# Making the first tail slot's first layer in the last steps of an attention loop

## The chip, the cores and the metric

The kernel runs on one core of one Trainium2 chip. The metric is the device time of one execution in microseconds (us); the time given for a kernel is the median of its runs. Engines are called as in the profile: PE (TensorE matmul), PEld (its weight loads), DVE (VectorE), ACT (ScalarE), POOL (GpSimd), SP (SyncE, here only a DMA queue).

## The reference, cut to what matters

Attention over 8 batches of 8 heads, 576 tokens and 64 columns a head, in which each row keeps its 32 largest scores; then a mixture of 8 experts over the 4608 tokens of 512 columns, one expert for each token.

```python
scores = scale * np.matmul(q, k.transpose(0, 1, 3, 2))
kth = np.partition(scores, -top_k, axis=-1)[..., -top_k:-top_k + 1]
scores = np.where(scores >= kth, scores, -1e9)
attn = softmax(scores) ; x = np.matmul(attn, v) as [4608, 512]
logits = x @ w_gate + modality_bias[modality_id]
e_idx = np.argmax(logits, axis=1)
for e in range(E):                       # E = 8, w1[e] is 512 x 1024, w2[e] 1024 x 512
    h = np.maximum(x[mask] @ w1[e], 0.0)
    out[mask] = gate_w[mask, None] * (h @ w2[e])
```

## The kernel before, in words

**One software pipeline over 288 score tiles.** A step `i` of the loop at L1123 works on nine stages of different tiles of 128 x 576 scores: the scores of tile i+2 (`qk`, L437), the search for the 32nd largest value (L452 to L498), the exponential (`expo`, L503), `keep` (L509, on DVE, tile i-7), the transposes `trans` (L524) and their copy `evac` (L532, tile i-9) and, three times in nine steps, the product with v (`av`, L552, copied at L556). NT is 288, QL is 2, TL is 9; the loop has 310 steps. The last scores are issued in step 285, the last `trans` in step 296, the last `av` in step 297. Steps 299 to 309 hold only what makes the last batch's routing.

**Routing of the last batch**, by steps: gate logits on PE in step 299 (`logits`, L606), their copy on ACT at the head of step 300 (L607), transposes in step 300 (`logit_rows`, L615), DVE reductions in step 301 (L618 to L626), then the list of `route` (L629) with up to four small operations a step from step 302 (L666 to L685; `ranks`, L642, has PE, ACT, POOL and DVE work), `xrow` (L588, copied by ACT at L596, multiplied on POOL at L592) in steps 302 to 306. From step 309 the rows are sent to their experts' lists in DRAM by five indirect DMAs on POOL (`send`, L659, tensor `xs`).

**Experts come in slots of 256 rows.** Slots 0 to 11 are worked in the loop by a list of PE items with costs (`expert`, L814; `moe` holds them): first layer `hid` (L859), second layer `outp` (L871, 16 items of 0.88). A budget `spare_pe` gains 3.25 in each step (`STEP`, L31), less the step's own cost, and items are issued while it is above zero (L1221 to L1241). The gain falls to 1.0 from step NT+TL+END[0] on (L66, L1221). Between slots, `turns` (L798, PE at L807) may transpose the next slot's rows early.

**Seven tail slots (12 to 18) follow the loop.** They multiply in three rounded terms: weights and rows are split into a high and a low part by `parts` (L1013: ACT copy at L1015, DVE subtraction at L1016). `first` (L1121) holds the five pieces that slot 12 needs ahead: four `split_w1` and one `turn_rows` (L1026, PE at L1031); before, they go out in steps 299 to 303, after `open_tail` (L994, step 298) has closed the pools of the attention and opened the pool of the tail. `slot(n)` (L1060) works slot n-1: eight pieces of the first layer (twelve matmuls each at L1069, then ACT L1071 and DVE L1072, and at every second piece `split_w2`), the loads of slot n's weights and rows (`load_w1` L790, `fetch` L1049, whose DMA is L771), the second layer's first half (L1087), then `turn_rows(n)`, `choose(n + 1)`, and the second layer's second half. The rows that `fetch` reads for slot 13 are in `xs`, so they need the sends of the last batch, and slot 13's expert is chosen (`choose`, L1043) after the routing.

**Order.** The program is scheduled by hand: each engine's queue has its instructions in the order in which the Python text issues them. SP has all weight and row loads in one queue. PSUM tiles named X rotate through three buffers, E has one.

Of the kernel before, what the change touches and what calls it, by code (L numbers as in the profile page):

```python
# [9 lines left out]
FT = mybir.dt.float32  # L10
FR = mybir.dt.float32r
BF = mybir.dt.bfloat16
I32 = mybir.dt.int32
AF = mybir.ActivationFunctionType
# [8 lines left out]
ME = 11  # L23
# [39 lines left out]
RXM = (5, 6, 7, 8, 9)  # L63
EZP = 1
RKP = 0
END = (-3, 1.0)  # L66
BIG = float(2.0 ** 100)
EPS = 1e-9
KTH_MIN, KTH_MAX = 1e-18, float(2.0 ** 26)
# [5 lines left out]
def kernel(  # L75
# [33 lines left out]
    att = ExitStack()  # L109
    ld = att.enter_context(tc.tile_pool(name="ld", bufs=2))  # L110
    wk = att.enter_context(tc.tile_pool(name="wk", bufs=3))

    ZROW = E * LCAP
    xs = dr.tile([ZROW + SLOT, XW], FT, name="xs")
# [14 lines left out]
    def load(p, what, b=None, queues=(SP, SP, SP), bufs=None):  # L129

        o = LD.setdefault(p, {})
        h0 = 2 * (p % HP)
        for nm in what:
            src = {"k": k, "q": q, "v": v}[nm]
            g = src[p // HP] if b is None else src[ds(b, 1)].rearrange("o h s d -> (o h) s d")
            if nm == "k":
                o["kq"] = bufs["kq"] if bufs else ld.tile([128, 2, D], FT, name="kqt", bufs=1)
            t = vtb[p % 2] if nm == "v" else o["kq"][:64] if nm == "k" else o["kq"][64:]
            m = bufs[nm] if bufs else ld.tile([128, 2, 4, D] if nm == "v" else [128, 4, 2, D], FT, name=nm + "m", bufs=2 if nm == "v" else 1)
            if nm == "v":  # L140
                SP.dma_start(m.rearrange("p h c d -> p h (c d)"),
                             g[h0:h0 + 2, 0:512, :].rearrange("h (p c) d -> p h (c d)", c=4))
            else:
                for h in range(2):
                    queues[h].dma_start(m[:, :, h, :], g[h0 + h, 0:512, :].rearrange("(p c) d -> p c d", c=4))
            if nm == "v":
                tail = g[h0:h0 + 2, 512:, :].rearrange("h p d -> p h d")
                SP.dma_start(t[:64, 0:3:2, :], tail)
                SP.dma_start(t[64:, 1, :], g[h0 + 1, 512:, :])
            else:  # L150
                queues[2].dma_start(t, g[h0:h0 + 2, 512:, :].rearrange("h p d -> p h d"))
            o[nm] = (m, t)
# [136 lines left out]
    def new_st():  # L289

        if not stt:
            stt.append(wk.tile([128, 2, 2, S], FR, name="st", bufs=1))
        return stt[0]

    def keep_st(f, w, c):
# [43 lines left out]
    def stacks(p, part, late):  # L339

        d = PR[p]
        if part == "k":
            d["ks"] = wk.tile([128, 2, 2, S], FR, name="ks", bufs=2)
        else:
            d["qs"] = wk.tile([128, 2, S], FR, name="qs", bufs=2)
        for h in range(2):
            late.append(lambda h=h: stack(p, part, h))

# [22 lines left out]
    def first_pair():  # L371

        d = PR.setdefault(0, {})
        st = d["st"] = new_st()
        (km, kt), (qm, qt) = LD[0]["k"], LD[0]["q"]
        pk, pa, pq = (psX.tile([128, 512], FT, name="X") for _ in range(3))

        def turn(ps, a, m, first=False, rows=slice(0, 128)):
            PE.matmul(ps[:, a:a + rows.stop - rows.start], m, idf[rows, rows], start=first, stop=False,
                      is_transpose=True, skip_group_check=True)  # L380

        def cut(which, a, b, ps):
            hi, lo = (st[:, x, which, a:b] for x in range(2))
            A.activation(hi, ps, AF.Copy)
            V.tensor_tensor(lo, ps, hi.bitcast(FT), op=OP.subtract)

        for c in range(4):
            turn(pk, c * 128, km[:, c], c == 0)
        idle_work(4)
        turn(pa, 0, qm[:, 0], True)  # L390
        turn(pa, 128, kt, rows=slice(0, 64))
        cut(0, 0, 512, pk)
        cut(1, 0, 128, pa[:, :128])
        cut(0, 512, S, pa[:, 128:192])
        for c in range(1, 4):
            turn(pq, c * 128 - 128, qm[:, c], c == 1)
        turn(pq, 384, qt, rows=slice(64, 128))
        d["ks"] = wk.tile([128, 2, 2, S], FR, name="ks", bufs=2)
        d["qs"] = wk.tile([128, 2, S], FR, name="qs", bufs=2)
        return lambda: cut(1, 128, S, pq[:, :S - 128])  # L400

    def first_stacks():
# [591 lines left out]
    def open_tail():  # L994

        nonlocal att, wk, gt, tk
        att.close()
        att = ExitStack()
        wk = att.enter_context(tc.tile_pool(name="tl", bufs=1))
        for t, nm, shape in ((w1s, "w1", [128, KC, F]), (w2s, "w2", [128, FC, Dm]), (xgs, "xg", [128, KC, SLOT]),  # L1000
                             (hs, "h", [128, FC, SLOT])):
            t.extend(wk.tile(shape, FR, name=nm + x) for x in "hl")
        gt = wk.tile([128, 2], FT, name="gt")
        tk = const.tile([128, 2], I32, name="tk")

    TERMS = ((0, 0), (0, 1), (1, 0))
    turn = [0]
# [47 lines left out]
    def put(t, ot):  # L1055
        apart(G.indirect_dma_start(  # L1056
            out=out[:, :], out_offset=bass.IndirectOffsetOnAxis(ap=tk[:, t:t + 1], axis=0),
            in_=ot, in_offset=None, bounds_check=N - 1, oob_is_err=False), outs)

    def slot(n, between=None, early=None):  # L1060

        if last:
            last.pop()()
        of_rows(n - 1)
        for f in range(FC):
            ps = acc([128, SLOT])
            for c in range(KC):
                for x, (a, b) in enumerate(TERMS):
                    PE.matmul(ps, w1s[a][:, c, f * 128:(f + 1) * 128], xgs[b][:, c, :],  # L1069
                              start=(c == 0 and x == 0), stop=(c == KC - 1 and x == 2))  # L1070
            A.activation(hs[0][:, f, :], ps, AF.Relu)  # L1071
            V.scalar_tensor_tensor(hs[1][:, f, :], ps, 0.0, hs[0][:, f, :].bitcast(FT), op0=OP.max, op1=OP.subtract)  # L1072
            if f % 2 == 0:
                split_w2(f // 2)
            if f == 0:
                for g in range(4):
                    load_w1(n, g)
                fetch(n)
            if f % 2 == 0:
                load_w2(n, f // 2)  # L1080
        if early:
            early()
        for t in range(2):
            py = acc([128, Dm])
            for f in range(FC):
                for x, (a, b) in enumerate(TERMS):
                    PE.matmul(py, hs[a][:, f, t * 128:(t + 1) * 128], w2s[b][:, f, :],  # L1087
                              start=(f == 0 and x == 0), stop=(f == FC - 1 and x == 2))
                if t == 0 and f % 2 == 1:
                    split_w1(f // 2)  # L1090
            ot = ol if t else const.tile([128, Dm], FT, name="ot", bufs=2)
            A.activation(ot, py, AF.Copy, scale=gt[:, t:t + 1])
            if t == 1:
                last.append(lambda: put(1, ot))
            else:
                put(0, ot)
                if between:
                    between()
                turn_rows(n)
                choose(n + 1)  # L1100
# [19 lines left out]
    rows_of = {}  # L1120
    first = deque([lambda g=g: split_w1(g) for g in range(4)] + [lambda: turn_rows(nslot[0])])  # L1121
    weaving[0] = True
    for i in range(LAST):  # L1123
        if 12 <= i < 12 + 2 * E and i % 2 == 0:
            pad_rows((i - 12) // 2)
# [94 lines left out]
            keep_warm(NW)  # L1220
        spare_pe = min(spare_pe + (STEP if i < NT + TL + END[0] else END[1]) - cost, CAP)  # L1221
        while seen[0] and spare_pe > 0:
            if i < NT + ME:
                more_moe()
            o = SL.get(nslot[0])
            if i < NT + ME and plan["ready"] == nslot[0] and plan["go"] and 0 < len(moe) <= TA and "rowed" in o and "px" not in o:
                o["px"] = None
                turnq.extend(turns(nslot[0]))
            if turnq and (not turnq[0][2] or taken[0] <= 2 - ranking[0]):
                c, f, new = turnq.popleft()  # L1230
                f()
                spare_pe -= c
                continue
            if not moe:
                break
            c, f, new = moe[0]
            if taken[0] > 2 - ranking[0] if new == 2 else new and after:
                break
            moe.popleft()
            f()  # L1240
            spare_pe -= c  # L1241
# [68 lines left out]
            x[0] -= 1  # L1310
        while puts and puts[0][0] <= 0:
            puts.popleft()[1]()
        if i == NT + OPEN:
            open_tail()
        if i > NT + OPEN and first and plan["ready"] == nslot[0] and len(moe) < (16 if len(first) > 1 else 6):
            first.popleft()()
    weaving[0] = False
    chores()
    while rush:
# [59 lines left out]
    with ExitStack() as nest:  # L1379
        for x in range(MAXSLOT):  # L1380
            nest.enter_context(tc.If(nrem > x))
            slot(S0 + 3 + x)
    att.close()


    att = ctx.enter_context(ExitStack())
# [3 lines left out]
    def slow_tile(j, dn):  # L1390
# [12 lines left out]
        A.activation(ex, t["S"], AF.Exp, bias=nm_)  # L1403
        probs(j)
        V.scalar_tensor_tensor(t["P"], t["S"], m[:, 31:32], ex, op0=OP.is_ge, op1=OP.mult, accum_out=dn)

    def slow():
        Pb[:] = [wk.tile([128, 2 * S], FT, name=f"P{i}", bufs=1) for i in range(2)]
# [77 lines left out]
```

## Time and profile before

| what | value |
|---|---|
| median of 3 runs | 1245.73 us (1243.84 to 1247.1) |
| profiled execution, its own time | 1242.61 us |
| span of the profiled execution | 1240.7 us |
| mean granted TensorE clock | 0.986 |
| PE busy, PEld busy | 1176.3 us (95%), 927.6 us (75%) |
| DVE busy | 1148.1 us (93%) |
| ACT busy | 1015.7 us (82%) |
| POOL busy | 614.5 us (50%) |

The span is what lies between the first and the last instruction; the execution's time has 1.9 us around it. Shares are means over the whole span, which has an attention part (to about 1047 us), the routing of the last batch and the tail slots (1060 to 1226 us). A row of a timeline gives start, length, engine, line, operation, the tiles written and read, and in brackets the idle time before it with what ended it. Matmul records overlap, since their ends are modelled: the time that a run of matmuls takes is read from start to start.

### The profile page before, as it was taken

Reading aid. Unit: us, or ns where it says so; the run is one execution under the profiler, and the core shown is the slowest. Engines: PE = TensorE matmul, PEld = TensorE weight load, DVE = VectorE, ACT = ScalarE, POOL = GpSimd, SP = SyncE. Lnnn points to the kernel's source line nnn. Section 1 sums busy time; section 2 is a strip of 40 time slices with the busy share of each in tenths; the row PEclk is TensorE's granted clock in tenths of the full one; section 3 lists DMA queues with packets and bytes.
Section 4 is the critical chain, followed back from the end, with each engine's and each line's share of the span. In section 5 each row is a group of like instructions: output and inputs, shape, how many; then the busy total and the mean of one; then the engine's idle time right before and its main releaser. Section 6 shows DMA issues by size and latency. Waiting matters only on the chain. (4 is left out here: it accounts for less than half of the span.)

```text
span 1240.7 us, 29108 instructions
## 1 busy us (share of the span) xinstructions
PE 1176.3 (95%) x8149; PEld 927.6 (75%) x8149; DVE 1148.1 (93%) x5829; ACT 1015.7 (82%) x2044; POOL 614.5 (50%) x1054
## 2 busy tenths in 40 slices
PE   7789988899999999999999999999999999899995
PEld 6677766777767687877868687777868785799894
DVE  6999999999999999999999999999999995867763
ACT  4899988888889998899988998899889986456453
POOL 3444447445664566456754585556555662511111
PEclk8999989999999999999999999999999999999998
DMA  6687644645466456666476466756675434667563
GB/s 145 175 237 191 152 105 125 212 134 164 95 204 188 123 160 201 179 159 168 106 223 187 108 188 185 199 146 180 174 201 156 116 117 146 207 243 259 182 234 112
DMA packets 214421, 210.52 MB, mean 170 GB/s; under 512 B 108605, under 2 KB 157757, under 8 KB 214240
## 3 DMA queue, kind: packets, MB, share of 16 engines
q1 hardware_dynamic: 206672, 188.33, 54.3%
q0 software_dynamic: 6208, 19.54, 4.3%
q8 instruction: 70, 1.15, 0.4%
q14 instruction: 111, 0.91, 0.2%
q10 hardware_dynamic: 1360, 0.59, 0.2%
HBM read 130.43 MB, written 28.95 MB: 128 GB/s over the span
## 5 line engine op out<-in xcount | busy, mean ns | idle before, releaser
L452 DVE MAX8 cand<-Ssb 128x8 f32<-128x82 f32 (+1 forms) x2016 | 429.2, 230 | 7.6 <-ACT Ssb L445 7.6
L485 POOL TENSOR_TENSOR y<-Ssb,K 128x576 f32<-128x576 f32 x288 | 367.1, 1275 | 9.5 <-ACT K L479 9.0
L437 PE MATMUL S<-ks,qs 128*128 128x288 f32 x1016 | 232.3, 351 | 31.1 <-ACT Ssb L445 22.0
L445 ACT ACTIVATE Ssb<-S 128x576 f32<-128x576 f32 (+1 forms) x289 | 190.0, 658 | 71.8 <-PE S L437 56.4
L479 ACT ACTIVATE K<-Ssb,mg 128x576 bf16<-128x576 f32 x288 | 228.5, 793 | 6.0 <-POOL y L485 5.6
L503 ACT ACTIVATE ex<-Ssb,mg 128x576 f32<-128x576 f32 x288 | 227.1, 789 | 0.3 <-POOL mg L470 0.3
L437 PEld LDWEIGHTS S<-ks,qs 128*128 128x128 f32 x1016 | 157.5, 191 | 89.3 <-issue 37.1
L513 POOL TENSOR_SCALAR spare<-P 1x1 f32<-1x1 f32 x256 | 47.1, 184 | 342.6 <-DVE mg L463 326.8
L489 DVE MAX8 mg<-y 128x8 f32<-128x576 f32 x288 | 214.4, 745 | 0.9 <-POOL y L485 0.9
L509 DVE SCALAR_TENSOR_TENSOR P<-Ssb,kth,ex 128x576 f32<-128x576 f32 x256 | 211.4, 826 | 2.2 <-ACT ex L503 1.9
L532 ACT ACTIVATE PT<-T 128x640 f32<-128x640 f32 (+1 forms) x288 | 192.2, 667 | 8.6 <-PE T L524 8.6
L859 PE MATMUL E<-xgT,w1b 128*128 128x256 f32 x768 | 187.8, 385 | 3.0 <-ACT hT L863 1.3
L871 PE MATMUL E<-w2b,hT 128*128 128x512 f32 x384 | 184.8, 602 | 1.0 <-ACT ot L881 0.5
L524 PE MATMUL T<-idf,P 128*128 128x128 f32 x1152 | 169.4, 274 | 0.0
L859 PEld LDWEIGHTS E<-xgT,w1b 128*128 128x128 f32 x768 | 137.8, 190 | 28.3 <-ACT hT L863 3.0
L552 PE MATMUL X<-PT,vm 128*64 128x256 f32 (+1 forms) x1536 | 148.3, 336 | 4.2 <-issue 2.7
L524 PEld LDWEIGHTS T<-idf,P 128*128 128x128 f32 x1152 | 135.8, 140 | 4.2 <-issue 1.7
L552 PEld LDWEIGHTS X<-PT,vm 128*64 128x64 f32 x1536 | 86.3, 138 | 51.1 <-issue 19.1
L871 PEld LDWEIGHTS E<-w2b,hT 128*128 128x128 f32 x384 | 65.5, 190 | 52.9 <-issue 47.5
L592 POOL TENSOR_TENSOR x<-x,rd 128x256 f32<-128x256 f32 (+1 forms) x80 | 52.2, 659 | 30.1 <-ACT x L596 27.4
L479 ACT ACTIVATION_READ_ACCUMULATOR K<-Ssb,mg 128x1 f32 x288 | 62.3, 216 | 0.0
L463 DVE MAX8 mg<-cand 128x8 f32<-128x56 f32 x288 | 61.2, 213 | 0.2
(213 smaller groups left out, 2184.9 us busy)
## 6 DMA issues: line engine op xcount, KB each, us to landing
w1b<-in_moe_w_dram SPq DMA_DIRECT2D x80, 512.0 KB, 5.5
w2b<-in_moe_w_dram SPq DMA_DIRECT2D x80, 512.0 KB, 4.7
ks<-st SPq DMA_DIRECT2D x56, 288.0 KB, 3.6
qs<-st SPq DMA_DIRECT2D x110, 144.0 KB, 2.7
ks<-st SPq DMA_DIRECT2D x54, 256.0 KB, 4.8
xg<-xs SPq DMA_DIRECT2D x20, 516.0 KB, 5.4
vm<-in_v_dram SPq DMA_DIRECT2D x32, 256.0 KB, 4.5
km<-in_k_dram SPq DMA_DIRECT2D x55, 128.0 KB, 4.1
```

Of the source, the lines that this page charges most:

```text
L437: PE.matmul(ps[:, hf, u - a:v - a], l, d["ks"][:, x, h, u + o:v + o], start=(n == 0), stop=(n == len(terms) - 1), skip_group_check=(j == 8))
L452: return [lambda s=s: V.max(c[:, s * 8:s * 8 + 8], T[i]["S"][:, bnd[s]:bnd[s + 1]]) for s in range(NSUB)]
L479: A.activation(t["K"], t["S"], AF.Sign, scale=-1.0 - 2.0 ** -23, bias=t["mg"][:, x, 23:24], accum_out=t["n"][:, x:x + 1])
L485: G.tensor_tensor(t["y"], t["S"], t["K"], op=OP.mult)
L489: V.max(t["mg"][:, i % 3, 24:32], t["y"])
L503: A.activation(t["ex"], t["S"], AF.Exp, bias=t["mg"][:, i % 3, 0:1])
L509: V.scalar_tensor_tensor(t["P"], t["S"], kth[:, i:i + 1], t["ex"], op0=OP.is_ge, op1=OP.mult, accum_out=dn)
L524: PE.transpose(T[i]["pt"][:, x, :], (Pm if c == 4 else Pb[c % 2])[:, h * 512 + x * 128:h * 512 + x * 128 + 128], idf)
L532: A.activation(o, T[i]["pt"][:, :n], AF.Copy)
L552: PE.matmul(o.rearrange("p (a b) -> p a b", a=2) if j < 8 else o, l, r, start=(c == 0), stop=(c == 4), skip_group_check=True)
L859: PE.matmul(ps[:, f % 2], w1b[:, c, f * 128:(f + 1) * 128], xgT[:, c, :], start=(c == 0), stop=(c == KC - 1))
L871: PE.matmul(o["py"], hT[:, f, t * 128:(t + 1) * 128], w2b[:, f, :], start=(f == 0), stop=(f == FC - 1))
```

## The change

Tiles from which q and k are made (`kqt`, `km`, `qm`, `st`, `ks`, `qs`) move into a pool `pp` of their own at the right end of memory. After step NT-QL (286) `open_right` closes it and opens `tr` there, with the rounded w1 and rows of the tail slots. The five pieces of `first` may go out from step 287 on, one a step, once slot 12 is planned, fewer than 16 items of `moe` are left and no load is queued. When `first` and `moe` are empty, one piece of slot 12's first layer, `hidden(f)`, is issued at the end of each step after step 298; `slot` then skips those that were made. The gain of 3.25 lasts through step 298 (`END`). The early `turns` of a slot are tried only before step 286, and no new slot is planned once `first` has begun.

```diff
-END = (-3, 1.0)
+END = (2, 1.0)
...
+    make = ExitStack()
+    pp = make.enter_context(tc.tile_pool(name="pp", bufs=1, side="right"))
...
-            stt.append(wk.tile([128, 2, 2, S], FR, name="st", bufs=1))
+            stt.append(pp.tile([128, 2, 2, S], FR, name="st", bufs=1))
...
-        wk = att.enter_context(tc.tile_pool(name="tl", bufs=1))
-        for t, nm, shape in ((w1s, "w1", [128, KC, F]), (w2s, "w2", [128, FC, Dm]), (xgs, "xg", [128, KC, SLOT]),
-                             (hs, "h", [128, FC, SLOT])):
+        wk = att.enter_context(tc.tile_pool(name="tl", bufs=1, reuse_waits="tile"))
+        for t, nm, shape in ((w2s, "w2", [128, FC, Dm]), (hs, "h", [128, FC, SLOT])):
...
+    def open_right():
+
+        make.close()
+        tr = make.enter_context(tc.tile_pool(name="tr", bufs=1, side="right", reuse_waits="tile"))
+        for t, nm, shape in ((w1s, "w1", [128, KC, F]), (xgs, "xg", [128, KC, SLOT])):
+            t.extend(tr.tile(shape, FR, name=nm + x) for x in "hl")
...
+    def hidden(f):
+        ps = acc([128, SLOT])
+        for c in range(KC):
+            for x, (a, b) in enumerate(TERMS):
+                PE.matmul(ps, w1s[a][:, c, f * 128:(f + 1) * 128], xgs[b][:, c, :],
+                          start=(c == 0 and x == 0), stop=(c == KC - 1 and x == 2))
+        A.activation(hs[0][:, f, :], ps, AF.Relu)
+        V.scalar_tensor_tensor(hs[1][:, f, :], ps, 0.0, hs[0][:, f, :].bitcast(FT), op0=OP.max, op1=OP.subtract)
+        if f % 2 == 0:
+            split_w2(f // 2)
...
-            if i < NT + ME:
+            if not first_begun[0]:
                 more_moe()
...
-            if i < NT + ME and plan["ready"] == nslot[0] and plan["go"] and 0 < len(moe) <= TA and "rowed" in o and "px" not in o:
+            if i < NT - QL and plan["ready"] == nslot[0] and plan["go"] and 0 < len(moe) <= TA and "rowed" in o and "px" not in o:
...
+        if i == NT - QL:
+            open_right()
         if i == NT + OPEN:
             open_tail()
-        if i > NT + OPEN and first and plan["ready"] == nslot[0] and len(moe) < (16 if len(first) > 1 else 6):
-            first.popleft()()
+        if i > NT - QL and first and plan["ready"] == nslot[0] and len(moe) < 16 and not (bulk or chore):
+            if len(first) > 1 or plan["go"]:
+                first_begun[0] = True
+                first.popleft()()
+        elif i > NT + OPEN and not (first or moe or after or bulk or chore) and made[0] < FC:
+            hidden(made[0])
+            made[0] += 1
```

## Rows read from the trace of the kernel before

**Rows 1.** Windows: busy us (x instructions) by engine, PEclk, DMA share, GB/s

```profile
1045.00:1060.00 15.00, 9.94 (x98) 6.43 (x95) 10.39 (x21) 8.92 (x18) 5.99 (x8) 0.98 0.25 86
...
1120.00:1140.00 20.00, 20.00 (x127) 18.03 (x126) 14.07 (x32) 10.85 (x17) 2.17 (x4) 1.00 0.56 194
```

**Rows 2.** Timeline of PE, from the last batch's routing to slot 13's rows

```profile
1047.16 1.18 PE L606 MATMUL X<-xT,wgt 128*32 128x512 f32 x16
1049.24 0.77 PE L615 MATMUL X<-idf,x 128*128 128x128 f32 x5 [0.91 <-ACT x L607]
...
1059.24 0.19 PE L646 MATMUL X<-ohb,tri 128*128 128x40 bf16 x1 [2.01 <-DVE ohb L674]
...
1060.20 0.56 PE L1069 MATMUL X<-xgh,w1h 128*128 128x256 f32 x1
...
1079.37 0.66 PE L1031 MATMUL E<-idf,xg 128*128 128x128 f32 x4 [0.84 <-DMA xg<-xs]
```

**Rows 3.** Waits of SP's queue, 1030 to 1095 us: total us, times, longest us

```profile
SPq L771 <- DMA xs<-x,dest: 7.1, 1, 7.1
```

**Rows 4.** Timeline of PE, steps 291 and 292

```profile
1031.21 1.04 PE L807 MATMUL X<-idf,xg 128*128 128x128 f32 x8
1032.08 1.88 PE L871 MATMUL E<-w2b,hT 128*128 128x512 f32 x4
1033.80 0.60 PE L524 MATMUL T<-idf,P 128*128 128x128 f32 x4
```

**Rows 5.** Timeline of DVE: the last two `keep`

```profile
1035.38 0.82 DVE L509 SCALAR_TENSOR_TENSOR P<-Ssb,kth,ex 128x576 f32<-128x576 f32 x1 [1.90 <-ACT ex L503]
...
1037.86 0.82 DVE L509 SCALAR_TENSOR_TENSOR Pm<-Ssb,kth,ex 128x576 f32<-128x576 f32 x1 [1.65 <-ACT ex L503]
```

**Rows 6.** Windows, L1069 alone, first two pieces: PE, PEld busy, PEclk, DMA share, GB/s

```profile
1060.20:1062.81 2.61, 2.61 (x12) 2.61 (x13) 0.52 0.02 6
1062.81:1064.24 1.43, 1.43 (x14) 1.43 (x13) 1.00 0.00 0
```

**Rows 7.** Timeline of ACT: the logits' copy, and operations of the first layer

```profile
1047.65 1.06 ACT L1015 ACTIVATE w1h<-w1b 128x1024 fp32r<-128x1024 f32 x1
1048.61 0.69 ACT L607 ACTIVATE x<-X 128x512 f32<-128x512 f32 x2
...
1063.01 0.38 ACT L1071 ACTIVATE hh<-X 128x256 fp32r<-128x256 f32 x1 [1.77 <-PE X L1069]
1063.29 1.05 ACT L1015 ACTIVATE w2h<-w2b 128x1024 fp32r<-128x1024 f32 x1
```

**Rows 8.** Timeline of DVE: routing of the last batch, and operations of the first layer

```profile
1051.43 0.48 DVE L623 TENSOR_TENSOR lt<-X,rd 128x128 f32<-128x128 f32 x2
...
1052.92 1.48 DVE L1016 TENSOR_TENSOR w1l<-w1b,w1h 128x1024 fp32r<-128x1024 f32 x1
1054.33 0.61 DVE L666 TENSOR_TENSOR r_l<-lgb,bias_all 128x40 f32<-128x40 f32 x1
...
1055.69 1.21 DVE L1016 TENSOR_TENSOR w1l<-w1b,w1h 128x1024 fp32r<-128x1024 f32 x1
...
1058.03 0.53 DVE L671 SCALAR_TENSOR_TENSOR r_key<-r_z,rev 128x40 f32<-128x40 f32 x1
...
1059.04 0.15 DVE L674 TENSOR_TENSOR ohb<-r_key,r_km 64x8 bf16<-64x8 f32 x1
...
1060.62 0.20 DVE L655 TENSOR_REDUCE r_ps<-r_pr 128x5 f32<-128x40 f32 x1 [0.83 <-POOL r_pr L680]
...
1065.87 1.20 DVE L1016 TENSOR_TENSOR w2l<-w2b,w2h 128x1024 fp32r<-128x1024 f32 x1
...
1071.27 0.42 DVE L1072 SCALAR_TENSOR_TENSOR hl<-E,hh 128x256 fp32r<-128x256 f32 x1
```

**Rows 9.** Timeline of POOL: the last product and the first send

```profile
1063.24 0.61 POOL L592 TENSOR_TENSOR x<-x,rd 64x256 f32<-64x256 f32 x1
1064.01 1.06 POOL L659 DMA_INDIRECT xs<-x,dest  x1 [0.17 <-issue]
```

More of the change, by code (lines that the diff above doesn't have):

```diff
@@ L136, in load @@
             if nm == "k":
-                o["kq"] = bufs["kq"] if bufs else ld.tile([128, 2, D], FT, name="kqt", bufs=1)
+                o["kq"] = bufs["kq"] if bufs else pp.tile([128, 2, D], FT, name="kqt", bufs=1)
             t = vtb[p % 2] if nm == "v" else o["kq"][:64] if nm == "k" else o["kq"][64:]
-            m = bufs[nm] if bufs else ld.tile([128, 2, 4, D] if nm == "v" else [128, 4, 2, D], FT, name=nm + "m", bufs=2 if nm == "v" else 1)
+            m = (bufs[nm] if bufs else ld.tile([128, 2, 4, D], FT, name="vm", bufs=2) if nm == "v" else
+                 pp.tile([128, 4, 2, D], FT, name=nm + "m", bufs=1))
             if nm == "v":
@@ L342, in stacks @@
         if part == "k":
-            d["ks"] = wk.tile([128, 2, 2, S], FR, name="ks", bufs=2)
+            d["ks"] = pp.tile([128, 2, 2, S], FR, name="ks", bufs=2)
         else:
-            d["qs"] = wk.tile([128, 2, S], FR, name="qs", bufs=2)
+            d["qs"] = pp.tile([128, 2, S], FR, name="qs", bufs=2)
         for h in range(2):
@@ L397, in first_pair @@
         turn(pq, 384, qt, rows=slice(64, 128))
-        d["ks"] = wk.tile([128, 2, 2, S], FR, name="ks", bufs=2)
-        d["qs"] = wk.tile([128, 2, S], FR, name="qs", bufs=2)
+        d["ks"] = pp.tile([128, 2, 2, S], FR, name="ks", bufs=2)
+        d["qs"] = pp.tile([128, 2, S], FR, name="qs", bufs=2)
         return lambda: cut(1, 128, S, pq[:, :S - 128])
@@ L1058, in put @@
             in_=ot, in_offset=None, bounds_check=N - 1, oob_is_err=False), outs)
+    def hidden(f):
[8 more added lines that the diff above has]
+            split_w2(f // 2)
+    made = [0]
     def slot(n, between=None, early=None):
@@ L1065, in slot @@
         for f in range(FC):
[L1066 to L1074, printed above, removed]
+            if f >= made[0]:
+                hidden(f)
             if f == 0:
@@ L1080, in slot @@
                 load_w2(n, f // 2)
+        made[0] = 0
         if early:
@@ L1122 @@
     weaving[0] = True
+    first_begun = [False]
     for i in range(LAST):
@@ L1383 @@
     att.close()
+    make.close()
     att = ctx.enter_context(ExitStack())
@@ L1405, in slow_tile @@
         V.scalar_tensor_tensor(t["P"], t["S"], m[:, 31:32], ex, op0=OP.is_ge, op1=OP.mult, accum_out=dn)
+    pp = wk
     def slow():
```

## The prediction, made before the changed kernel was run

> **What bounds the kernel now.** I looked first at windows of the end of the run. In a tail slot PE is busy for all of 20 us, at full clock; between 1045 and 1060 us, while the last batch is routed, it is busy for 9.94 of 15 us [rows 1]. So there are 5.1 us of gaps, just ahead of a stretch that is all PE. Then I read PE's timeline through the gaps and on to the next break. After the gaps PE goes straight from the routing into slot 12's first layer at 1060.20, and later it stops once more: at 1079.37 it waits 0.84 us for `xg`, the rows of slot 13 [rows 2]. This row decides the case. Up to there PE's work is covered by another chain, which ends last: logits, reductions, ranks, `dest`, five sends into `xs`, `fetch` of slot 13's rows. SP's waits name its last link: the load waits 7.1 us for the sends [rows 3]. So the end of the run is the landing of slot 13's rows plus a fixed rest (half of slot 12's second layer, then slots 13 to 18), and PE work taken out of 1060 to 1079 us gives nothing unless these rows land sooner. The question is what the change does to the chain from the logits to `dest`.
>
> **The change, part by part.** The sum is made in the profiled execution, 1242.61 us with a span of 1240.7; it lies 3.1 us under the median of the three runs, 1245.73, to which I add the sum at the end.
>
> *Pools and waits.* The last scores are issued in step 285, so nothing holds the new pool when `first` starts. I take 0.
>
> *Order up to step 298.* `moe` has 13 items left after step 289, so the four `split_w1` go out in steps 289 to 292 and `turn_rows` in 293. Without L807 and with 3.25 a step, the 16 items end in step 294 (3, 3, 3, 1, 3, 3), where before two were left for steps 300 and 302.
>
> *Start of the logits, +2.3.* An item takes half of 1033.80 - 1032.08, 0.86 us, so two items more ahead of the logits are 1.72; `turn_rows` has the same eight transposes as L807, which goes (1032.08 - 1031.21 = 0.87), so these cancel [rows 4]. DVE gets four subtractions of 1.21, and two of `xg` (with one of w1 they fill 1055.69 to 1058.03, so 1.13 for the two), 6.0 us, ahead of the last `keep` [rows 8]; that one and the one before it have 3.55 us of idle time to give [rows 5]. PE alone gives 1.7, DVE alone would move the last `keep` by 2.4 to 6 us, while its transposes come 1.7 us later anyway. I take 2.3, near PE's end, with 1.7 and 4.0 as ends.
>
> *The chain inside steps 299 to 306.* Every step now ends with a piece of the first layer: twelve matmuls, 1.43 us at full clock [rows 6], then on ACT 0.38 and on DVE 0.42, and at each second piece 1.05 on ACT and 1.20 on DVE [rows 7, 8]. Queues keep the order of the text: the copy of the logits starts at 1048.61, only when the split ahead of it is over [rows 7]. So an operation of step 300 waits on its engine for the piece of step 299, which itself waits for PE and ACT. I laid the queues out link by link, and each difference to before is this:
> - Logits to their copy on ACT: before 1048.61 - 1047.16 = 1.45 [rows 2, 7]. After: logits 1.1, matmuls 1.43, hand-over 0.2, ACT 0.38 and 1.05, together 4.15. +2.7.
> - Transposes to the first DVE product: before 1051.43 - 1049.24 = 2.2 [rows 2, 8], since DVE was in a split. After: transposes 0.55, matmuls 1.43, ACT 0.38, DVE 0.42, hand-overs 0.2. +0.8.
> - Reductions to `l2`: before 1.41, a split of w1. After: a subtraction of 0.42 and one of 1.20, with 0.2 of waiting. +0.4.
> - `z` to `key`: before `key` starts 2.34 after 1055.69, behind a split and two row subtractions [rows 8]. After: one 0.42. -1.9.
> - `oh`: before its last part runs at once, at 1059.04, and the ranks follow at 1059.24 [rows 2, 8]. After, a part of w2 stands between: 1.05 on ACT behind the piece's matmuls, then 1.20 on DVE, and hand-overs. +2.5.
> - Ranks to `total` (L655): before 1060.62 - 1059.24 = 1.4, and DVE waits there for POOL [rows 2, 8]. After, DVE must first finish steps 304 and 305: two pieces (2 x 1.43 on PE, with two `xrow`s of 0.5, one X buffer that waits 0.8 for ACT's copy, ACT 0.38 and 1.05, DVE 1.20) and the small ones, 7.5 in all. +6.1. This is the largest term; were only DVE's own times in the way (2 x 0.42 and 1.20), it would be +2.0.
> - `total` to the last product on POOL: before 1060.62 to 1063.24 [rows 8, 9]; after, the last `xrow` is copied behind the last piece's ACT work. +0.8.
>
> The chain's sum is 2.7 + 0.8 + 0.4 - 1.9 + 2.5 + 6.1 + 0.8 = 11.4, with the start 13.7. Sends and load, from the first send at 1064.01 to slot 13's transposes at 1079.37 [rows 2, 9], move as a block: slot 13's weights are chosen behind `dest` and loaded beside the sends in both kernels. So slot 13's transposes start at 1079.37 + 13.7 = 1093.1.
>
> *PE meanwhile.* Its pieces end near 1074, the first half of the second layer near 1080 (24 matmuls), then it waits some 12 us. After a wait it restarts slowly: the first twelve matmuls at 1060.20 took 2.61 us at a clock of 0.52, the next twelve 1.43 [rows 6]. That 1.2 us lay beside the chain before; now it lies on the path. +1.2, with 0 and 2.4 as ends.
>
> Sum: 13.7 + 1.2 = 14.9 us; 1257.5 for the profiled execution, 1260.6 against the median.
>
> **The rivals.**
>
> *A, not slower: the pieces fall into PE's gaps.* The five parts of `first` leave the routing, which takes out of the chain ACT's 0.3 ahead of the logits' copy and DVE's 1.4, 1.41 and 2.34: 5.4 us. If the pieces then delay no link, the rows land 2.3 - 5.4 = 3.1 us sooner: 1242.6. It decides at `total` (L655): it has to run before 1060.6. For it: PE's gaps are there [rows 1]. Against it: text order puts each piece ahead of the next step's link, on three engines. If PE's ledger decided, the gain would be gaps 5.1, slow clock 1.2, wait 0.84 and L807 0.87, 8 us: 1237.7. The Trainium skill (Perfetto Trace Analysis, Identifying the Most-Contended Engine) would side with this: judge PE by its weight-load share and work first on the engine that is fullest. Here that share is 18.03 of 20 us in a tail slot [rows 1], so the rule holds there; the wait for `xg` [rows 2] speaks against it at the one place that counts. Chance 0.08, of which 0.05 is faster by over 0.3%.
>
> *B, slower by less: the engines' own times only.* The pieces' matmuls overlap the links, and the chain grows by the start (2.3) and by DVE's own time: eight times 0.42 and four times 1.20, 8.2, in place of the 6.0 that leave. That is +4.5, 1250.2; with part of the lock-step, up to 1255. Chance 0.18.
>
> *C, slower by more: PE at half clock in the pieces.* PE would be busy some three quarters of the time there; if the clock falls, each of the five pieces on the path takes 1.18 more [rows 6], 5.9 in all: 1266.5, and with the upper end of the start 1268.2. Chance 0.09.
>
> *D, the pieces are not made in the loop.* If a queued load holds `first` past step 298, `hidden` starts late and what is left is made after the loop, as before. The start's 2.3 and the links' gain then nearly cancel: 1245. Chance 0.04, nearly all of it within 0.3%.
>
> **How the numbers follow.** My forecast, the lock-step at full clock, has 0.61 and lies between 1255 and 1266; its own lower end is `total` at +2.0 instead of 6.1 and no slow restart, 1255.3. The range for 8 in 10 goes from B's 1250 to 1267, below C's upper end; A, D and a part of C are left out. A measurement of this kernel can tell about 0.3% (3.7 us) from no change. Faster by that: 0.05 from A. Within: 0.03 of A, 0.03 of D. Slower: 0.89.
>
> **What the profile would show.** Right: L607 some 4 us behind the logits, with pieces of L1069's matmuls between them in the routing; `total` near 1074; the last send near 1084; at slot 13's transposes PE idle some 12 us for the DMA of `xg`, and a granted clock near half in the first us behind it; no L807 for slot 12. Wrong: if `total` runs before 1062, if PE does not wait at slot 13's transposes, or if the pieces stand behind the routing.

## The result, and the profile after

The changed kernel takes 1260.92 us (median of 5 runs, 1258.33 to 1262.55); the kernel before took 1243.84 us beside it (5 runs, 1241.93 to 1247.1). The medians lie 17.1 us apart. The ratio of the runs is 1.0129 with a 95% interval of 1.0117 to 1.0142, which is 16.0 us slower (14.6 to 17.7). The forecast was 1260.6 us, from a sum of 14.9 us.

The profiled execution of the changed kernel took 1262.55 us, with a span of 1260.7 us. It is the slowest of the five, and the profiled execution of before lies 1.2 us under its median, so the two spans differ by 20.0 us and not by 17.1. PE's timeline, from tile 280's transposes to slot 13's first layer (start in us, duration of the group, then engine, line and operation; lines of the changed kernel):

```profile
1027.97 0.71 PE L527 MATMUL T<-idf,P 128*128 128x128 f32 x5
...
1053.57 1.18 PE L609 MATMUL X<-xT,wgt 128*32 128x512 f32 x16
...
1058.31 0.77 PE L618 MATMUL X<-idf,x 128*128 128x128 f32 x5 [1.96 <-ACT x L610]
...
1071.15 0.18 PE L649 MATMUL X<-ohb,tri 128*128 128x40 bf16 x1 [2.73 <-DVE ohb L677]
...
1095.37 1.12 PE L1040 MATMUL E<-idf,xg 128*128 128x128 f32 x4 [10.99 <-DMA xg<-xs]
...
1104.21 0.28 PE L1073 MATMUL X<-xgh,w1h 128*128 128x256 f32 x1
```

Against [rows 2]: the logits start at 1053.57 instead of 1047.16, the ranks at 1071.15 instead of 1059.24, slot 13's transposes at 1095.37 instead of 1079.37, and PE waits there 10.99 us for the rows instead of 0.84. The chain between, on ACT, DVE and POOL; first ACT:

```profile
1056.44 0.38 ACT L1075 ACTIVATE hh<-X 128x256 fp32r<-128x256 f32 x1 [2.54 <-PE X L1073]
1056.72 1.05 ACT L1024 ACTIVATE w2h<-w2b 128x1024 fp32r<-128x1024 f32 x1
1057.67 0.70 ACT L610 ACTIVATE x<-X 128x512 f32<-128x512 f32 x2
```

The logits' copy (L610) stands behind the first piece's ACT operation and the first rounding of w2, 4.10 us after the logits; before it was 1.45 us [rows 2, 7]. Then DVE, from the first product to `total` (the row of `r_l` is the prediction's `l2`, that of `r_key` its `key`):

```profile
1061.61 0.42 DVE L1076 SCALAR_TENSOR_TENSOR hl<-E,hh 128x256 fp32r<-128x256 f32 x1 [2.58 <-ACT hh L1075]
1061.95 0.48 DVE L626 TENSOR_TENSOR lt<-X,rd 128x128 f32<-128x128 f32 x2
...
1065.99 0.19 DVE L669 TENSOR_TENSOR r_l<-lgb,bias_all 128x40 f32<-128x40 f32 x1
...
1067.24 0.32 DVE L674 SCALAR_TENSOR_TENSOR r_key<-r_z,rev 128x40 f32<-128x40 f32 x1
...
1069.38 1.23 DVE L1025 TENSOR_TENSOR w2l<-w2b,w2h 128x1024 fp32r<-128x1024 f32 x1 [0.52 <-ACT w2h L1024]
1070.52 0.57 DVE L677 TENSOR_TENSOR ohb<-r_key,r_km 64x8 bf16<-64x8 f32 x1
...
1076.35 1.22 DVE L1025 TENSOR_TENSOR w2l<-w2b,w2h 128x1024 fp32r<-128x1024 f32 x1 [0.52 <-ACT w2h L1024]
...
1077.59 0.16 DVE L658 TENSOR_REDUCE r_ps<-r_pr 128x5 f32<-128x40 f32 x1
```

Each link stands right behind a piece's subtraction: `lt` behind the second piece's `hl`, `ohb` and `total` (L658) behind roundings of w2, while DVE stands idle ahead of the pieces' operations, 2.58 us at the longest, waiting for their PE and ACT parts. `total` comes at 1077.59, where [rows 8] have 1060.62. POOL's first send follows 2.5 us later, right behind the last of POOL's products:

```profile
1078.18 1.77 POOL L595 TENSOR_TENSOR x<-x,rd 128x256 f32<-128x256 f32 x3
1080.11 1.06 POOL L662 DMA_INDIRECT xs<-x,dest  x1 [0.16 <-DVE tbl L756]
```

The products end at 1079.95. In every profile of this document the first send starts 0.16 to 0.17 us behind them, so the chain into the sends passes through ACT's row copies and these products as well as through `total`. From the first send to slot 13's transposes are 15.26 us, 15.36 before [rows 2, 9]. Last, windows of the stretches that matter (columns as in [rows 1]):

```profile
1060.00:1065.00 5.00, 5.00 (x33) 5.00 (x33) 2.41 (x8) 1.71 (x3) 0.00 (x0) 0.70 0.00 0
1085.00:1090.00 5.00, 0.00 (x0) 0.00 (x0) 1.23 (x1) 1.49 (x2) 1.42 (x6) 0.69 1.00 325
1095.00:1100.00 5.00, 4.63 (x15) 4.05 (x16) 3.63 (x16) 1.19 (x2) 1.39 (x2) 0.50 0.97 304
1095.37:1104.21 8.84, 8.84 (x33) 7.43 (x33) 4.50 (x24) 1.19 (x2) 1.19 (x2) 0.71 0.86 281
1120.00:1140.00 20.00, 20.00 (x140) 18.58 (x139) 12.84 (x32) 9.68 (x18) 3.48 (x6) 1.00 0.62 221
```

PE does nothing from 1085 to 1090, restarts at a granted clock of 0.50, and is as full in a tail slot as it was in [rows 1]. The eight transposes of slot 13 and the 24 matmuls behind them take 8.84 us here. Before, they took 6.42 us at full clock:

```profile
1079.37:1085.79 6.42, 6.42 (x33) 5.44 (x33) 4.94 (x24) 1.09 (x2) 1.62 (x2) 1.00 0.94 327
```

The 20.0 us between the two spans, each stretch from the rows of both (tile 280's transposes before, then the last copy on ACT before and after):

```profile
1024.12 0.71 PE L524 MATMUL T<-idf,P 128*128 128x128 f32 x5
...
1226.00 0.69 ACT L1092 ACTIVATE otl<-X,gt 128x512 f32<-128x512 f32 x1 [4.68 <-issue]
...
1244.49 0.69 ACT L1108 ACTIVATE otl<-X,gt 128x512 f32<-128x512 f32 x1 [4.68 <-issue]
```

| stretch | before | after | difference | forecast |
|---|---|---|---|---|
| to tile 280's transposes | 1024.12 | 1027.97 | 3.9 | 0 |
| from there to the logits | 23.04 | 25.60 | 2.6 | 2.3 |
| logits to slot 13's transposes | 32.21 | 41.80 | 9.6 | 11.4 |
| these transposes and the half behind them | 6.42 | 8.84 | 2.4 | 1.2 |
| from there to the last copy on ACT | 140.21 | 140.28 | 0.1 | 0 |
| last copy to the end of the span | 14.7 | 16.2 | 1.5 | 0 |

The three stretches that the change touches by the forecast make 14.6 us. The other 5.4 us, at the start and at the very end, are taken up below, with the kernel without pieces, with the pools alone and with a second profile of before.

### The profile page after: what moved, and what is told of

Same layout as the page of the kernel before. It is cut to its first block, busy times and chain, and to the rows that moved or that the text cites. A ratio compares the mean times of both kernels' runs of the same rounds, so it can differ in the third digit from the quotient of the medians.

```text
span 1260.7 us, 29078 instructions
## 1 busy us (share of the span) xinstructions
PE 1180.5 (94%) x8141; PEld 932.3 (74%) x8141; DVE 1148.7 (91%) x5829; ACT 1013.0 (80%) x2042; POOL 609.9 (48%) x1054
## 5 line engine op out<-in xcount | busy, mean ns | idle before, releaser
L482 ACT ACTIVATE K<-Ssb,mg 128x576 bf16<-128x576 f32 x288 | 228.4, 793 | 5.4 <-POOL y L488 5.0
L482 ACT ACTIVATION_READ_ACCUMULATOR K<-Ssb,mg 128x1 f32 x288 | 62.3, 216 | 0.0
```

Source lines behind the costliest of these rows:

```text
L482: A.activation(t["K"], t["S"], AF.Sign, scale=-1.0 - 2.0 ** -23, bias=t["mg"][:, x, 23:24], accum_out=t["n"][:, x:x + 1])
```

## The experiments

The theory: pieces of the first layer, put in text order between the links of the last batch's routing, hold up these links on PE, ACT and DVE in turn, and the rows of slot 13 come late by as much. The rivals: the early splits, the budget or the pools cost the time; PE's matmuls alone set the pace; PE's sum of work decides; each piece has its price wherever it stands. Medians are compared with the runs of before made beside them (1243.9 to 1244.1 us).

**No pieces in the loop.**

```diff
-        elif i > NT + OPEN and not (first or moe or after or bulk or chore) and made[0] < FC:
+        elif False and i > NT + OPEN and not (first or moe or after or bulk or chore) and made[0] < FC:
```

> The whole change, but no piece of slot 12's first layer is made in the loop; all eight follow it, as before. Theory (the pieces, put in text order between the links of the last batch's routing, hold up the chain to slot 13's rows): the start stays 2.3 us late, the splits have left the routing (up to 5.4 us), the rows land about 2 us sooner than before; 1241 to 1243 against 1243.8 before. Rival 1 (the early splits of w1, the budget or the new pools cost the time): 1255 or more, as little changes in those.

Measured: 1244.03 us, ratio 1.0001 (0.9992 to 1.0010). So the pieces in the loop are worth 17 us, all of the loss; the early splits, the budget and the pools together make nothing that can be told from zero. The gain of 2 us that was expected as well is not there in the time, though it is in the trace. PE's timeline of this kernel:

```profile
1053.34 1.18 PE L609 MATMUL X<-xT,wgt 128*32 128x512 f32 x16
...
1080.44 0.66 PE L1040 MATMUL E<-idf,xg 128*128 128x128 f32 x4 [2.08 <-DMA xg<-xs]
...
1086.82 0.28 PE L1073 MATMUL X<-xgh,w1h 128*128 128x256 f32 x1
```

DVE's timeline of the same kernel, at `total`:

```profile
1060.49 0.20 DVE L658 TENSOR_REDUCE r_ps<-r_pr 128x5 f32<-128x40 f32 x1 [0.47 <-POOL r_pr L683]
```

And POOL's, with the last products and the first send:

```profile
1063.10 1.76 POOL L595 TENSOR_TENSOR x<-x,rd 128x256 f32<-128x256 f32 x3
1065.03 1.06 POOL L662 DMA_INDIRECT xs<-x,dest  x1 [0.17 <-DVE s_sc L764]
```

From the logits to `total` are 7.15 us instead of 13.46 [rows 2, 8], but POOL's products end only at 1064.86, so the first send comes 4.5 us after `total` and not 3.4 us. From the logits to slot 13's transposes are 27.1 us against 32.2 before: 5.1 us less, of which the later start takes 2.6.

Between this profile (span 1243.4 us) and that of the whole change (1260.7) the account closes: 27.1 against 41.8 us from the logits to slot 13's transposes, 6.4 against 8.8 from there to slot 13's first layer, 14.7 and 2.5 us, together 17.2 of the 17.3 between the spans. The late start and end of the table above are in both, so the pieces do not make them.

**The rounding of w2 after the loop.**

```diff
-            hidden(made[0])
+            hidden(made[0], False)
...
             if f >= made[0]:
                 hidden(f)
+            elif f % 2 == 0:
+                split_w2(f // 2)
```

Here `hidden` has an argument that leaves out its `split_w2`.

> The pieces stay in the loop, but the rounding of w2 (four times 1.05 us on ACT and 1.20 on DVE) is made after the loop. Theory: each of these stands in text ahead of a link (logits' copy, l2, second part of oh, total), so dest comes 4.6 us sooner; 1256 against 1260.9. Rival 2 (PE's matmuls of the pieces set the pace, ACT and DVE ride along): under 1 us, 1260.

Measured: 1256.19 us, ratio 1.0105 (1.0090 to 1.0121), 4.7 us under the change by the medians and 3.0 by the ratios; the ranges of the runs do not overlap. From the logits to slot 13's transposes are 37.6 us instead of 41.8, by PE's timeline of this kernel:

```profile
1052.28 1.18 PE L609 MATMUL X<-xT,wgt 128*32 128x512 f32 x16
...
1089.90 0.66 PE L1040 MATMUL E<-idf,xg 128*128 128x128 f32 x4 [3.31 <-DMA xg<-xs]
```

That is 4.2 us less. The 4 x 1.05 us on ACT and 4 x 1.20 us on DVE do not ride along with the matmuls; rival 2 falls.

**The pools alone.** The edits of `END`, of both conditions in the PE budget and of the step that issues `first` are undone and no pieces are made, so that each engine has the order of before.

```diff
-END = (2, 1.0)
+END = (-3, 1.0)
...
-            if not first_begun[0]:
+            if i < NT + ME:
...
-            if i < NT - QL and plan["ready"] == nslot[0] and ...
+            if i < NT + ME and plan["ready"] == nslot[0] and ...
...
-        if i > NT - QL and first and ...
+        if i > NT + OPEN and first and ... and len(moe) < (16 if len(first) > 1 else 6):
```

> Order of every engine as before; only the tiles of q and k, w1 and rows lie in the new pools. Theory: nothing, 1243.8 within 0.3%. Rival 3 (the changed places in memory cost something over the whole attention; step 289 came 3.9 us later in the profile of the change): 1246 to 1248.

Measured: 1245.85 us, ratio 1.0008 (0.9998 to 1.0018), within 0.3% of before. It is also only 0.15 us short of rival 3's range, so a cost of the pools of up to 2.2 us is not excluded. In its profile, too, the logits come 4.3 us later than in [rows 2], and again nearly all of it arises at the start. It can be followed on ACT's sign operation of each score tile (L479 before, L482 after), a part of the search for the 32nd largest value: that of tile 0 is 2.2 us later than in the first profile of before, that of tile 10 by 3.4, that of tile 285 by 4.2. Between tile 10 and tile 285 the delay grows by 0.8 us; it grows by 0.6 in the second profile of before, which has the old places in memory. PE's timeline of this kernel, at the logits:

```profile
1051.48 1.18 PE L609 MATMUL X<-xT,wgt 128*32 128x512 f32 x16
```

**Both halves of the second layer ahead of slot 13's transposes**, in the first tail slot alone.

```diff
-                turn_rows(n)
-                choose(n + 1)
+                if not swap:
+                    turn_rows(n)
+                    choose(n + 1)
+        if swap:
+            turn_rows(n)
+            choose(n + 1)
```

> The whole change, but in the first tail slot both halves of the second layer stand ahead of slot 13's transposes. Theory (the end is the landing of slot 13's rows plus a fixed rest): the rest is one half, 24 matmuls of 0.229 us, 5.5 us, shorter, and the half that ran slowly after the wait now runs at full clock; 1254 to 1255.5. Rival 4 (PE's sum of work decides): no change, 1261.

Measured: 1256.05 us, ratio 1.0109 (1.0094 to 1.0125), 4.9 us under the change by the medians and 2.5 by the ratios, whose intervals overlap. The trace is clearer. PE's work is the same, only more of it stands ahead of the wait, and the wait is 5.3 us shorter, as PE's timeline of this kernel has it:

```profile
1094.80 1.97 PE L1040 MATMUL X<-idf,xg 128*128 128x128 f32 x8 [5.71 <-DMA xg<-xs]
1096.60 0.58 PE L1073 MATMUL X<-xgh,w1h 128*128 128x256 f32 x1
1097.33 0.58 PE L1073 MATMUL X<-xgl,w1h 128*128 128x256 f32 x1
```

ACT's last copy of this kernel:

```profile
1238.57 0.69 ACT L1109 ACTIVATE otl<-X,gt 128x512 f32<-128x512 f32 x1 [4.68 <-issue]
```

From slot 13's transposes to this copy are 143.8 us; in the whole change they are 149.1. So the end hangs on the landing of slot 13's rows; rival 4 falls. The time came out 0.5 us above the expected range. The slow restart, which the expectation did not count there, now falls on slot 13's first pieces, whose records are 0.58 us long at first, where they are 0.28 at full clock.

**Four pieces, first and late.** The same number of pieces in the loop, once the first four steps (299 to 302), once from step 306 on, behind `total` and `dest` in the text, but not behind ACT's copy of the last rows.

```diff
-        elif i > NT + OPEN and not (first or moe or after or bulk or chore) and made[0] < FC:
+        elif i > NT + OPEN and not (first or moe or after or bulk or chore) and made[0] < 4:
```

```diff
-        elif i > NT + OPEN and not (first or moe or after or bulk or chore) and made[0] < FC:
+        elif i > NT + OPEN + 7 and not (first or moe or after or bulk or chore) and made[0] < FC:
```

> The whole change, with only the first four pieces made in the loop (steps 299 to 302) and four behind it. Theory (place decides): ahead of the logits' copy, the first product and l2 these four cost 2.7 + 0.8 + 0.4, and the second part of w2 delays oh no more; 8 us over the kernel without pieces (1244.0), 1250 to 1253. Beside it stands the kernel with four pieces from step 306 on, 1248.0. Rival (a share of the cost for each piece, wherever it stands): both alike.

> The whole change, but the pieces start in step 306, whose list has the last operations of the routing (total, dest); four are made in the loop, four behind it. Theory (the place among the links is the cost): 0 to 2 us over the kernel without pieces in the loop, 1244 to 1246. Rival (each piece made early costs its share of the 17 us): half of it, 1252.

Measured: 1255.19 us (ratio 1.0093, 1.0076 to 1.0110) with the first four, 1247.98 us (1.0031, 1.0019 to 1.0042) with the late four. Over the kernel without pieces that is 11.2 and 4.0 us, 2.8 and 1.0 a piece: the place decides, and neither is half of the 17 us. Both came out some 2 us above what was expected. PE's timeline with the first four:

```profile
1051.07 1.18 PE L609 MATMUL X<-xT,wgt 128*32 128x512 f32 x16
...
1087.13 1.12 PE L1040 MATMUL E<-idf,xg 128*128 128x128 f32 x4 [7.62 <-DMA xg<-xs]
...
1095.45 0.28 PE L1073 MATMUL X<-xgh,w1h 128*128 128x256 f32 x1
```

36.1 us from the logits to slot 13's transposes against 27.1 without pieces, and 1.9 us of slow restart. With the late four the links up to `total` are as quick as without any (7.1 us from the logits). But the first send comes 5.5 us behind `total` instead of 4.5. ACT's copy of the last rows stands behind the first late piece's operation and rounding, and POOL waits 0.24 us for it; the two products behind that wait took 1.89 us, where the last three took 1.76 us without pieces. By ACT's and POOL's timelines of that kernel:

```profile
1062.75 1.05 ACT L1024 ACTIVATE w2h<-w2b 128x1024 fp32r<-128x1024 f32 x1
1063.70 0.58 ACT L599 ACTIVATE x<-X 64x512 f32<-64x512 f32 x1
...
1064.35 1.89 POOL L595 TENSOR_TENSOR x<-x,rd 64x256 f32<-64x256 f32 x2 [0.24 <-ACT x L599]
1066.41 1.06 POOL L662 DMA_INDIRECT xs<-x,dest  x1 [0.16 <-DVE hl L1076]
```

From the logits to slot 13's transposes this kernel takes 27.7 us, 0.6 more than without pieces. Another 1.3 us is the restart behind a wait of 3.42 us, as its PE timeline shows; the other 2 us of the 4.0 do not show in these two profiles:

```profile
1053.77 1.18 PE L609 MATMUL X<-xT,wgt 128*32 128x512 f32 x16
...
1081.47 1.12 PE L1040 MATMUL E<-idf,xg 128*128 128x128 f32 x4 [3.42 <-DMA xg<-xs]
...
1089.19 0.28 PE L1073 MATMUL X<-xgh,w1h 128*128 128x256 f32 x1
```

**Toward a version that beats both.** First the budget of before (`END = (-3, 1.0)`) without pieces in the loop; then also both halves ahead of the transposes (`swap` where `n == S0 + 1`); then on top of that two pieces in steps 303 and 305 with w2 rounded after the loop; then, without those two, three pieces ahead of the choice of slot 13 behind the loop.

```diff
-        elif i > NT + OPEN and not (first or moe or after or bulk or chore) and made[0] < FC:
+        elif i in (303, 305) and not (first or moe or after or bulk or chore) and made[0] < FC:
```

```diff
+    while made[0] < 3:
+        hidden(made[0])
+        made[0] += 1
     choose(S0 + 1)
```

> No pieces in the loop, and the budget falls to 1.0 at step 294 as before, so one or two items of the second layer stand behind the logits again. Theory: the logits start up to 1.7 us sooner than without pieces alone (1244.0), and slot 13's rows with them: 1242 to 1242.5. Rival (PE is ahead of the rows by nothing any more, its sum decides): 1244.

> No pieces in the loop, old budget, and in the first tail slot both halves of the second layer stand ahead of slot 13's transposes. Theory: PE now reaches the rows 5.5 us later and they have landed by then, so the wait of some 2 us goes and PE's own work decides: 1 to 2 us under the same kernel with the old order of the halves, 1240 to 1241.5. Rival (the rest is fixed): the full 5.5 us, 1237.

> As the kernel with both halves ahead of slot 13's transposes, with two pieces of the first layer made in steps 303 and 305, at the ends of steps whose next link waits for another engine anyway, and all rounding of w2 after the loop. Theory: the rows come up to 2 us later, which PE's 5.5 us of work ahead of them covers, and 1 to 1.5 us of PE's gaps are filled: 1239 to 1240. Rival (any piece among the links costs): 1242 or more.

> As the kernel without pieces in the loop, old budget, and both halves ahead of slot 13's transposes, with the first three pieces of the first layer issued ahead of the choice of slot 13 behind the loop, so that their subtractions on DVE do not stand behind its twenty small operations. Theory: PE's wait of 1.5 us for a subtraction goes, and slot 13's weights come some 3 us later without being waited for: 1241, 1.5 us under that kernel. Rival (the choice is itself on the chain that ends last, through slot 13's weights): 1242.4 or more.

Measured, as ratios to before: 0.9993 (0.9984 to 1.0002) with the old budget, 1243.53 us; 0.9987 (0.9978 to 0.9996) with both halves ahead, 1242.41 us; 0.9989 (0.9980 to 0.9998) with two pieces, 1243.04 us; 0.9994 (0.9985 to 1.0002) with three pieces ahead of the choice, 1243.19 us. By these ratios the second and the third are faster than both kernels, by 1.6 and 1.4 us: their intervals end just short of 1, and both gains are under 0.3%. The theory's expectations were about 1 us (budget), 1 us, 3 us and 2 us too good. The rivals of the first, third and fourth run named a time near the measured one or a bound that it keeps (1244; 1242 or more; 1242.4 or more); only that of the second, 1237, is excluded. With the old budget, PE's matmuls behind the wait for slot 13's rows also ran at a lower clock than without pieces alone: the eight transposes and 24 matmuls took 8.01 us at 0.79, against 6.38 us at 1.00, by windows of the two kernels and PE's timeline of the old budget (the columns of windows are those of [rows 1]; the first window is of the kernel without pieces alone):

```profile
1080.44:1086.82 6.38, 6.38 (x32) 5.44 (x33) 4.22 (x24) 1.09 (x2) 1.00 (x2) 1.00 0.96 327
...
1077.23:1085.24 8.01, 8.01 (x32) 6.59 (x33) 3.95 (x21) 1.08 (x2) 0.66 (x2) 0.79 0.90 309
...
1077.23 0.66 PE L1040 MATMUL E<-idf,xg 128*128 128x128 f32 x4 [1.99 <-DMA xg<-xs]
```

In the second run PE no longer waits for the rows, by its timeline:

```profile
1065.83 0.39 PE L1073 MATMUL X<-xgh,w1h 128*128 128x256 f32 x1 [1.52 <-DVE hl L1076]
...
1082.78 1.04 PE L1040 MATMUL X<-idf,xg 128*128 128x128 f32 x8
```

The longest wait that is left there is one of 1.52 us for a subtraction, behind DVE's small operations of `choose`. With three pieces ahead of the choice it did not go but moved to a later piece, by PE's timeline of that kernel:

```profile
1070.63 0.38 PE L1073 MATMUL X<-xgh,w1h 128*128 128x256 f32 x1 [1.31 <-DVE hl L1076]
```

So no piece issued early, between the links or ahead of the choice, gained anything that could be told from none. PE's idle times from the logits on sum to 4.1 us in the second run and to 5.8 in the kernel before; whether the rest can be filled, no run shows.

**The kernel before, once more.**

> The kernel before once more, for a second profile. If the profiles of the variants are late by 0.1 to 2.7 us at tile 0, and end 1 us later behind the last copy, only by chance, this one can be anywhere in that spread too. If the pools cost it, tile 0 and the end are as in the first profile of before (0.0, and 6.0 us from the last copy to the last indirect DMA).

Measured: one time of 1243.46 us. Its sign of tile 0 is 0.6 us earlier than in the first profile, that of tile 285 0.3 us later. PE does not wait for slot 13's rows at all in it, by its timeline:

```profile
1079.52 0.64 PE L1031 MATMUL E<-idf,xg 128*128 128x128 f32 x4
```

So in the kernel before, PE and the chain reach this point together; the 0.84 us of [rows 2] is near the balance and not a fixed wait. In the ten variants above tile 285's sign is 0.8 to 4.2 us later than in the first profile. From the last copy's start to the last indirect DMA it has 6.7 us, the first profile 6.0, the variants 6.4 to 8.3. Both profiles of before lie at the low side of these spreads, which speaks for a small cost of the pools at the start. It would also fit the kernel without pieces, whose gain is in its trace and not in its time. But the interval of the pools alone includes zero, so this stays open.

## Why the prediction was right

- **What bounds the kernel.** The wait of 0.84 us for `xg` was read as the end of the chain that decides, and it was: with PE's work before it unchanged in sum, the wait grew to 10.99 us; more PE work moved ahead of it shortened the wait by 5.3 us and the stretch behind it as much.
- **Start of the logits**, 2.3 us forecast, 2.6 measured.
- **The links**, measured by the same rows (+ is later than before): logits to copy +2.65 (2.7 forecast), transposes to first product +1.45 (0.8), first product to `l2` +1.1 (0.4), `l2` to `key` -2.45 (-1.9), `key` to ranks +2.7 (2.5), ranks to `total` +5.1 (6.1), `total` to the first send -0.9 (+0.8); 9.6 in all, where 11.4 was forecast. Four terms were off, and their errors partly cancel. The second and the third were too small, as PE ran pieces at a granted clock of 0.70 between 1060 and 1065, a part of rival C that the forecast had at full clock. The sixth was 1 us too large. The last had the wrong sign: `total` came so late that POOL's products ended only 2.4 us behind it, where it was 3.2 us before; without pieces they ended 4.4 us behind it, and the send came 1.1 us later after `total` than before. Since the send waits for these products too, the sixth and the last are best read together, from the ranks to the first send: +4.2 measured, +6.9 forecast.
- **The restart**, forecast at 1.2 us with 2.4 as its end, measured 2.4: the eight transposes and 24 matmuls took 8.84 us after a wait of 10.99 us, against 6.42 after 0.84. The row it came from had twelve short matmuls at the low clock; here the transposes and eight of the 24 matmuls ran at it, until 1100.55.
- **The rivals.** A, not slower, fell with the measurement and by its own sign: `total` ran at 1077.59, not before 1060.6. The late four pieces and the two pieces in steps 303 and 305 gained nothing either. The rule of fullness by weight-load share (the Trainium skill, Perfetto Trace Analysis, Identifying the Most-Contended Engine) did not decide here: that share is about as high as before in a tail slot, 18.58 of 20 us, and the time is 17 us longer. B, the engines' own times only, ended at 1255 and falls with the time, and with DVE's rows: it stands idle between the links for the pieces' PE and ACT parts. The rounding of w2 moved out does not separate B from lock-step, since DVE's own part of it, 4 x 1.20, is 4.8 us, as much as the measured 4.7. C, half clock in five pieces, came in part: the second and the third piece took 2.12 and 2.32 us from start to start instead of 1.43, 1.6 us in all, not 5.9. D did not occur, since all eight pieces stand among the routing's rows.
- **The sum.** 14.9 us were forecast; the medians differ by 17.1 and the ratio stands for 16.0. That 1260.6 us came within 0.3 us of the measured 1260.92 is luck: the median it started from, 1245.73 us, was 1.9 us above that of the runs beside the changed kernel, and the sum was 2.2 us too small. The three stretches that were worked out have 14.6 us in the profile, with the chain 1.8 us below its forecast and the restart 1.2 us above. The rest is at the start and end of the run, which the kernel without pieces shares; its cause is not shown.

## What to carry to other kernels

Before work is moved into an engine's gaps, find out what ends the next wait of that engine: here PE's gaps were the outside of a chain through ACT, DVE and POOL, and whatever is issued between two links of such a chain is paid on each engine that it passes. A wait under 1 us behind a full stretch can be the row that decides, since it shows two chains in balance. When work has to be put beside a chain, its place counts: four pieces cost 2.8 us each at the chain's head and 1.0 each near its end, where they still stood ahead of one copy. Work that needs nothing from the chain can stand ahead of the wait for its result, as with both halves of the second layer.

## What the runs showed that was not expected

What PE's first work behind a wait costs follows the granted clock, and the length of the wait alone does not give it. Windows from slot 13's transposes to slot 13's first layer, over the same eight transposes and 24 matmuls in each kernel:

| kernel | wait before, us | these matmuls, us | granted clock |
|---|---|---|---|
| before | 0.84 | 6.42 | 1.00 |
| no pieces | 2.08 | 6.38 | 1.00 |
| no pieces, old budget | 1.99 | 8.01 | 0.79 |
| w2 rounded after the loop | 3.31 | 8.03 | 0.79 |
| late four pieces | 3.42 | 7.72 | 0.82 |
| first four pieces | 7.62 | 8.32 | 0.75 |
| the whole change | 10.99 | 8.84 | 0.71 |

After two waits of about 2 us the same work took 6.38 us in one kernel, all at full clock (2.4 GHz), and 8.01 us in another, where the clock was at the lower of its two levels (1.2 GHz) for a part of it. In the four rows below these a part ran at the lower level as well; behind the longest wait the clock was 0.50 from 1095 to 1100 us. Why the clock fell behind one wait of 2 us and not behind the other, no run here shows.
